# Moving the K, V and wq/wo slots below the constants in a decode-attention kernel

## The chip, the cores and the metric

The kernel runs on one core of a Trainium2 chip. The metric is the device time of one execution in microseconds (us), lower is better.

## What is computed

A decode step of a transformer block for 4 sequences with one token each, in bfloat16, with a width D of 640: attention over a cache of 4096 positions with 32 heads of 128, then a dense block with the Mish activation. Cut to what matters:

```python
q  = (layernorm(x) @ wq) as [4, 32, 1, 128]           # wq is 640 x 4096
p  = softmax(einsum("bhqd,bhkd->bhqk", q, k_cache) * 128**-0.5)
o  = einsum("bhqk,bhkd->bhqd", p, v_cache)             # caches are 4 x 32 x 4096 x 128
h  = x + o as [4, 1, 4096] @ wo                        # wo is 4096 x 640
f  = layernorm(h) @ w1 + b1                            # w1 is 640 x 1728
h2 = h + (f * tanh(log1p(exp(-|f|)) + max(f, 0))) @ w2 # w2 is 1728 x 640
```

The two caches are 134 MB each, read once. All the weights together are some 15 MB.

## The kernel before, in words

The attention is cut into 32 groups: group g is four heads (`hq = g // 4`) of one sequence (`b = g % 4`). The 128 partitions hold those four heads with 32 partitions each, and a partition holds 128 consecutive positions of its head (R = 128). So one group's K is a tile of 128 partitions with 128 x 128 bfloat16, which is one run of 32,768 bytes in each partition, and V has the same form. One DMA of 4096 KB loads such a tile (`load_kv`, L85 to L94, issued from the SP queue at L93); only the last group's K and V come in two halves.

For each group and each half of its positions, VectorE multiplies the K tile in place by the broadcast query in two passes (L334, in `mul_and_sum`), and TensorE adds up the products over the 128 columns with 32 matmuls against an identity (L341, 16 in each half). VectorE finishes the sum (L353) and TensorE, VectorE and ScalarE make the softmax (L360 to L391). Then TensorE multiplies V by the weights (`pv_moving`, L238 to L250, 32 matmuls at L242), one group behind. Between the groups stand the query projection (L185 to L211, for the first eight groups), the loads and products of wo (L426 to L434 and `project`, L311) and the bias. The order is written out by hand (`manual_schedule`, L73, and the loop from L394).

The K pool and the V pool have two slots each. The load of K for group g + 2 is issued when the multiplies and matmuls of group g have released their slot (L416), that of V for group g + 1 after L242 of group g - 1 (L422). All of them stand in one queue, SP's, in program order. wq and wo use one after the other the single slot of the pool `wbig` (L106 and L431, wo in four DMAs whose rows are 1280 bytes). After the last group, w1 and the larger part of w2 go into a slot of the K pool (L453 to L464), and a short chain of small operations makes the dense block and writes the output (L467 to L597).

Where a tile lies in a partition follows from the order in which the pools are made (L75 to L79): each pool begins where the one before it ends, and each tile is placed at the next multiple of 32 bytes. The first 16,384 bytes are reserved, four small built-in constants come next, and the first pool begins at byte 16,512. The pools come in the order `consts`, `wbig`, `work`, `kpool`, `vpool`, and the pool `mlp` is made last (L452). The built program before has these first bytes:

| tile | first byte in each partition | modulo 512 | modulo 64 |
|---|---|---|---|
| `ident` (L113) | 17,792 | 384 | 0 |
| `qbs` (L213), the broadcast query | 36,736 | 384 | 0 |
| wq/wo slot | 48,416 | 288 | 32 |
| K slots | 93,088 and 125,856 | 416 | 32 |
| V slots | 158,624 and 191,392 | 416 | 32 |

Of the kernel before, what the change touches and what calls it, by code (L numbers as in the profile page):

```python
# [9 lines left out]
BF16 = mybir.dt.bfloat16  # L10
# [6 lines left out]
def kernel(  # L17
# [54 lines left out]

    ctx.enter_context(tc.manual_schedule())  # L73

    consts = ctx.enter_context(tc.tile_pool(name="consts", bufs=1))  # L75
    wbig = ctx.enter_context(tc.tile_pool(name="wbig", bufs=1))
    work = ctx.enter_context(tc.tile_pool(name="work", bufs=2))
    kpool = ctx.enter_context(tc.tile_pool(name="kpool", bufs=KBUFS))
    vpool = ctx.enter_context(tc.tile_pool(name="vpool", bufs=VBUFS))  # L79

    x_rows = A_x.rearrange("b s d -> (b s) d")
    out_rows = out.rearrange("b s (c p) -> (b s c) p", p=128)
# [546 lines left out]
```

## Time and profile before

| what | value |
|---|---|
| median of three runs | 674.84 us (674.6 to 674.92) |
| the profiled execution, its own time | 674.36 us |
| its span, first to last instruction | 672.6 us |
| granted TensorE clock, mean | 0.935 |
| TensorE, VectorE, ScalarE busy | 566.7, 351.6, 112.2 us (84%, 52%, 17% of the span) |
| bytes read from HBM | 283.35 MB, 421 GB/s over the span |
| VectorE's longest single wait group: L334 for K loads | 222.8 us in 30 waits |

The profile gives busy times of the engines, the span cut into 40 slices, the DMA queues with their packets, the chain of waits that ended last, and groups of like instructions. A DMA is cut into packets, here one for each partition's contiguous run; the trace has a record of every packet with its start, its duration and its size. The share of a DMA queue is the time that its packets took as a share of 16 engines over the window, and can go slightly over 100% because one packet of an engine begins a little before the one before it ends.

### The profile page before, as it was taken

The numbers are of one execution on the slowest core, as the hardware profiler recorded it, in microseconds if no ns is written. First come the engines' busy times: TensorE is split into PE (matmuls) and PEld (weight loads), VectorE is DVE, ScalarE is ACT, GpSimd is POOL, SyncE is SP. The second block draws the span as 40 slices with busy tenths as digits, with TensorE's granted clock in tenths as the row PEclk, the third lists the DMA queues.
The fourth block names the chain that finished last, engine by engine and source line by source line (L and its number), as shares of the span: only waits on it lengthen the run. The fifth ranks groups of instructions, "written<-read, shape, count | busy, mean of one in ns | idle before, by whom it ended". The sixth has DMA issues, their size and how long they took to land.

```text
span 672.6 us, 7163 instructions
## 1 busy us (share of the span) xinstructions
PE 566.7 (84%) x3121; PEld 256.1 (38%) x3121; DVE 351.6 (52%) x304; ACT 112.2 (17%) x343; POOL 2.4 (0%) x13
## 2 busy tenths in 40 slices
PE   0589999899998896688999899879988799888985
PEld 0234444344443332233443344333433344333454
DVE  2475445455654356236654545665544566554642
ACT  0022122122210111011110111111111111101231
POOL 1000000000000000000000000000000000000000
PEclk9999999799998987878998899898999799898995
DMA  9999999999999999999999999999999999999995
GB/s 373 437 436 437 430 428 428 426 437 434 432 431 421 422 416 412 441 419 425 430 434 427 433 430 430 431 435 432 431 428 428 433 434 437 428 431 424 433 411 204
DMA packets 15191, 283.81 MB, mean 422 GB/s; under 512 B 1267, under 2 KB 5559, under 8 KB 6584
## 3 DMA queue, kind: packets, MB, share of 16 engines
q1 hardware_dynamic: 15152, 283.36, 98.8%
q8 instruction: 24, 0.39, 0.2%
q14 instruction: 7, 0.06, 0.0%
q10 hardware_dynamic: 8, 0.01, 0.0%
HBM read 283.35 MB, written 0.01 MB: 421 GB/s over the span
## 4 chain that ended last, share of the span: by engine, by line
DMA 43%; PE 37%; DVE 18%; issue 1%; ACT 1%; SPq 0%; DVEq 0%
DMA kt<-in_A_k_cache_dram 41%; PE s L341 19%; DVE kt L334 15%; PE p L242 11%; PE ot L256 3%; DMA vt<-in_A_v_cache_dram 3%; PE q_ps L188 1%; PE qb_ps L202 1%; DVE s_sb L353 1%; PE tr L366 1%; DVE mx L371 1%; ACT q_all L195 1%; PE h_ps L511 0%; PE l_ps L280 0%; PE y2T L573 0%
## 5 line engine op out<-in xcount | busy, mean ns | idle before, releaser
L334 DVE TENSOR_TENSOR kt<-kt,qbs 128x4096 bf16<-128x4096 bf16 x128 | 291.4, 2278 | 222.8 <-DMA kt<-in_A_k_cache_dram 222.8
L341 PE MATMUL s<-kt,ident 128*128 128x512 bf16 x1024 | 267.4, 408 | 75.8 <-DVE kt L334 75.6
L242 PE MATMUL p<-vt,e 128*16 128x512 bf16 x960 | 214.2, 382 | 0.0
L341 PEld LDWEIGHTS <-ident 128*128 128x128 bf16 x1024 | 99.7, 103 | 199.5 <-issue 100.6
L242 PEld LDWEIGHTS <-e 128*16 128x16 bf16 x960 | 84.3, 90 | 129.8 <-issue 17.8
L384 ACT ACTIVATE e<-s_sb,nbs 32x128 bf16<-32x128 f32 x128 | 73.9, 577 | 2.5
L250 ACT COPY p_sb<-p 16x512 f32<-16x512 f32 x30 | 17.2, 574 | 316.6 <-PE p L242 316.6
L353 DVE TENSOR_REDUCE s_sb<-s 128x64 f32<-128x512 f32 x64 | 43.4, 678 | 3.4 <-PE s L341 3.3
L381 ACT COPY nbs<-tr 128x4 f32<-128x4 f32 x32 | 5.2, 162 | 177.4 <-PE tr L379 177.4
L256 PEld LDWEIGHTS ot<-ident_f,p_sb 16*128 16x128 f32 x240 | 28.9, 186 | 12.7 <-issue 12.7
L384 ACT ACTIVATION_READ_ACCUMULATOR e<-s_sb,nbs 32x1 f32 x128 | 32.1, 251 | 0.0
L256 PE MATMUL ot<-ident_f,p_sb 16*128 16x4 f32 x240 | 31.5, 250 | 0.0
L371 DVE TENSOR_REDUCE mx<-tr 1x4 f32<-1x128 f32 x32 | 8.9, 277 | 41.4 <-PE tr L366 41.3
L188 PE MATMUL q_ps<-wq_sb,xT 128*4 128x512 bf16 x40 | 11.0, 409 | 9.7 <-DMA wq_sb<-in_A_wq_dram 9.7
L366 PE MATMUL tr<-ident_f,pm 128*1 128x128 f32 x64 | 13.7, 300 | 1.2 <-DVE pm L364 1.2
L379 PEld LDWEIGHTS tr<-mx,nscale 1*128 1x128 f32 x64 | 9.4, 182 | 13.8 <-issue 12.7
L288 DVE RECIPROCAL rl<-l_ps 128x16 f32<-128x16 f32 x8 | 2.1, 257 | 23.1 <-PE l_ps L280 23.1
L202 PE MATMUL qb_ps<-q_all,sel 4*128 4x128 bf16 x128 | 9.2, 225 | 5.3 <-ACT q_all L195 5.3
L379 PE MATMUL tr<-mx,nscale 1*128 1x4 f32 x64 | 12.2, 258 | 0.4 <-DVE mx L371 0.4
L202 PEld LDWEIGHTS <-sel 4*128 4x128 bf16 x128 | 8.4, 98 | 9.1 <-issue 9.1
L195 ACT CAST q_all<-q_ps 4x512 bf16<-4x512 f32 x8 | 4.6, 574 | 34.6 <-PE q_ps L188 34.6
L366 PEld LDWEIGHTS tr<-ident_f,pm 128*1 128x1 f32 x64 | 2.8, 81 | 18.4 <-issue 18.4
(79 smaller groups left out, 81.5 us busy)
## 6 DMA issues: line engine op xcount, KB each, us to landing
kt<-in_A_k_cache_dram SPq DMA_DIRECT2D x31, 4096.0 KB, 24.5
vt<-in_A_v_cache_dram SPq DMA_DIRECT2D x31, 4096.0 KB, 27.7
wq_sb<-in_A_wq_dram SPq DMA_DIRECT2D x1, 5120.0 KB, 15.3
wo_sb<-in_A_wo_dram SPq DMA_DIRECT2D x4, 1280.0 KB, 30.5
kt<-in_A_k_cache_dram SPq DMA_DIRECT2D x2, 2048.0 KB, 19.6
vt<-in_A_v_cache_dram SPq DMA_DIRECT2D x2, 2048.0 KB
w<-in_B_w_dram SPq DMA_DIRECT2D x1, 2160.0 KB, 22.9
w<-in_B_w_dram SPq DMA_DIRECT2D x3, 640.0 KB, 19.8
```

Source lines behind the costliest of these rows:

```text
L188: nc.tensor.matmul(q_ps[:, :], lhsT=xT[:, c, :], rhs=wq_sb[:, c, n * QC : (n + 1) * QC], start=(c == 0), stop=(c == DC - 1),)
L202: nc.tensor.matmul(qb_ps[:, b * Dh : (b + 1) * Dh], lhsT=sel[:, b, q, :], rhs=q_all[:, h * Dh : (h + 1) * Dh], start=(q == 0), stop=(q == ...
L242: nc.tensor.matmul(p_ps[:, :], lhsT=e2[g % NE2][:, r : r + J, :].rearrange("p j q -> p (j q)"), rhs=vt[:, r : r + J, :].rearrange("p j d - ...
L250: nc.scalar.copy(out=blocks[g][:, :], in_=p_ps[:, :])
L256: nc.tensor.matmul(o, lhsT=p_sb[:, j * Dh : (j + 1) * Dh], rhs=ident_f[0 : J * G, j * G : (j + 1) * G], start=(j == 0), stop=(j == J - 1),)
L334: nc.vector.tensor_tensor(out=kt[:, :, d0 : d0 + DQ], in0=kt[:, :, d0 : d0 + DQ], in1=qbs[:, hq, b, d0 : d0 + DQ].unsqueeze(1).to_broadcas ...
L341: nc.tensor.matmul(s_ps[:, :, :], lhsT=ident[:, :], rhs=kt[:, :, d : d + W], start=(d == 0), stop=(d == Dh - W),)
L353: nc.vector.tensor_reduce(out=s_sbs[g][:, part * RP : (part + 1) * RP], in_=s_of.pop((g, part))[:, :, :], axis=AX.X, op=ALU.add,)
L366: nc.tensor.matmul(tr_ps[0:1, 0:128], lhsT=pm[:, :], rhs=ident_f[:, :], start=True, stop=True)
L371: nc.vector.tensor_reduce(out=mx[:, :], in_=tr_ps[0:1, 0:128].rearrange("o (a b) -> o a b", a=G), axis=AX.X, op=ALU.max,)
L379: nc.tensor.matmul(nb_ps, lhsT=nscale[:, :], rhs=mx[:, :], start=True, stop=True)
L384: nc.scalar.activation(out=e2[g % NE2][p0:p1, :, q], in_=s_sb[p0:p1, :], func=ACT.Exp, bias=nb[p0:p1, q : q + 1], scale=SCALE, accum_out=r ...
```

## The change

Four things are done to the pools. An unused tile of 384 bytes in a new pool `pad` is made first. `kpool` and `vpool` follow, then `wbig`, then `consts`, then `work`; `mlp` is still the last. Nothing else is edited.

```diff
-    consts = ctx.enter_context(tc.tile_pool(name="consts", bufs=1))
-    wbig = ctx.enter_context(tc.tile_pool(name="wbig", bufs=1))
-    work = ctx.enter_context(tc.tile_pool(name="work", bufs=2))
+    pad = ctx.enter_context(tc.tile_pool(name="pad", bufs=1))
+    pad.tile([128, 192], BF16, name="pad")
     kpool = ctx.enter_context(tc.tile_pool(name="kpool", bufs=KBUFS))
     vpool = ctx.enter_context(tc.tile_pool(name="vpool", bufs=VBUFS))
+    wbig = ctx.enter_context(tc.tile_pool(name="wbig", bufs=1))
+    consts = ctx.enter_context(tc.tile_pool(name="consts", bufs=1))
+    work = ctx.enter_context(tc.tile_pool(name="work", bufs=2))
```

In the built program of the change the first bytes are these:

| tile | first byte in each partition | modulo 512 |
|---|---|---|
| K slots | 16,896 and 49,664 | 0 |
| V slots | 82,432 and 115,200 | 0 |
| wq/wo slot | 147,968 | 0 |
| `ident` | 190,208 | 256 |
| `qbs` | 209,152 | 256 |

## The prediction

> **What bounds the kernel now.** I read the DMA rows of the page first, since the kernel streams 283 MB and computes little on each byte. The first fence is the page: its two DMA lines in 40 slices, its SP queue, the loads of K and V.
>
> ```profile
> DMA  9999999999999999999999999999999999999995
> GB/s 373 437 436 437 430 428 428 426 437 434 432 431 421 422 416 412 441 419 425 430 434 427 433 430 430 431 435 432 431 428 428 433 434 437 428 431 424 433 411 204
> ...
> q1 hardware_dynamic: 15152, 283.36, 98.8%
> ...
> kt<-in_A_k_cache_dram SPq DMA_DIRECT2D x31, 4096.0 KB, 24.5
> vt<-in_A_v_cache_dram SPq DMA_DIRECT2D x31, 4096.0 KB, 27.7
> ```
>
> The 16 DMA engines are busy from the first slice to the last but one. A K load of 4096 KB needs 9.8 us at 430 GB/s, but lands 24.5 us after its issue: about 15 us of other loads stand ahead of it, so the queue doesn't run dry. The same by stages (columns: length; busy time and instructions of PE, PEld, DVE, ACT, POOL; granted clock; DMA share; GB/s):
>
> ```profile
> 26.00:44.00 18.00, 13.87 (x67) 5.84 (x67) 15.35 (x11) 1.16 (x2) 0.00 (x0) 1.00 1.00 433
> 50.00:125.00 75.00, 70.65 (x379) 32.51 (x378) 40.41 (x31) 16.87 (x48) 0.00 (x0) 1.00 1.00 429
> 330.00:600.00 270.00, 239.46 (x1167) 104.25 (x1166) 147.22 (x116) 42.73 (x140) 0.00 (x0) 0.95 1.00 431
> 656.00:672.00 16.00, 8.88 (x229) 8.24 (x229) 3.42 (x17) 2.00 (x4) 0.00 (x0) 0.50 0.57 208
> ```
>
> The DMA share is 1.00 wherever K and V stream, with VectorE busy for 15.35 of 18 us as well as with it half idle. Only from 656 us, after the last V, is it lower. Last, the chain of waits: early groups hold no DMA, one group following the other by TensorE at 19.2 us (50.60 to 69.81), so computing and DMA run at nearly one pace; later the chain waits for K.
>
> ```profile
> 50.60 7.00 PE p L242 x32
> ...
> 62.85 2.21 DVE kt L334
> 65.11 1.89 PE s L341 x8
> 66.99 0.98 PE ot L256 x8
> 67.97 1.83 PE s L341 x8
> 69.81 7.00 PE p L242 x32
> ```
>
> So the end is set by how long the 16 engines take over their packets, plus 16 us of tail.
>
> **The change, part by part.** *The programs.* In the built program of the change every engine has the same instructions in the same order with the same waits, SP's loads included; only addresses in SBUF differ. Nothing is moved past a queue, no wait is added, the unused tile takes no instruction. So only two prices can change: that of a packet's write, and that of an engine's read or write of a tile.
>
> *A packet's write.* K and V rows begin at 416 modulo 512 before and at 0 after; wq and wo at 288 before and 0 after. What does one packet cost beyond its bytes? The DMA view of 26 to 44 us, where the stream is undisturbed, says:
>
> ```profile
> DMA packets 267, 7.80 MB, mean 433 GB/s; under 512 B 29, under 2 KB 29, under 8 KB 29
> q1 hardware_dynamic: 267, 7.80, 100.3%
> ```
>
> 29 packets are the semaphores' (4 bytes, 9 ns each in the records of single packets), the other 238 are rows of 32,768 bytes: (1.003 x 16 x 18 us - 0.3 us) / 238 = 1,213 ns. The single records agree: until 44.7 us every row takes exactly 1,213 ns, and the 16,384-byte rows of the last halves take 611 ns at the least. The difference, 602 ns for 16,384 bytes, is 27.2 bytes per ns, so the bytes of a row alone need 1,204 ns. In one engine's sequence the next packet begins 1,210 ns after a row's start, 607 ns after a half row, 131.5 ns after a w1 row of 3,456 bytes (127 ns of bytes), and 6 ns after a semaphore packet. The cost beyond the bytes is 4 to 6 ns each time. It is no larger for the row that begins at 160 modulo 256 than for four bytes of semaphore, whose place the change doesn't touch. So I take the part that alignment could remove at **0 us**.
>
> The bound: all of some 5 ns goes. One engine has 7,936 / 16 = 496 whole rows, 512 / 16 = 32 half rows, 128 / 16 = 8 rows of wq, 4,096 / 16 = 256 of wo, and 40 + 24 of w1 and w2 (they lie in a K slot), together 856 packets; 856 x 5 ns = **4.3 us**, a gain of 0.64%. [...]
>
> The rows of w1 begin at 160 and 32 modulo 256 in turn, and the trace has runs of them at 135 ns each with starts 131 to 132 ns apart, whichever it is. [...]
>
> *Disturbed packets.* From 330 to 480 us whole rows take 1,218.6 ns on average, not 1,213. This begins with the first instruction load at 44.71 us and not with the computing, which starts at 25.87; in several stretches of single records every fourth packet of an engine is the long one, by some 7 ns, whatever its size. Neither speaks for a place in SBUF. I take no change. The 5.6 ns as a bound lie beside the 5 ns above: I don't add them.
>
> *The engines.* L334, L341 and L242 read the moved tiles. L334 has 2,278 ns for 4,096 columns, and the chain shows L341 at 1.83 us for 8 matmuls of 512 columns and L242 at 7.00 us for 32: 0.45 ns per column in the one, 0.43 in the other, though the first reads runs of 16 bytes at steps of 256 and the second whole rows. All start at a multiple of 32 bytes before and after. I take 0. The cover is the wait for K in the later groups (L334 waits 222.8 us for it) and, in the early ones, the 15 us of loads ahead of each load.
>
> *The tail.* Its small operations read constants and `mlp` tiles that lie elsewhere now; there is no DMA cover for them after 656 us. They have 8.88 + 3.42 + 2.00 = 14.3 us of busy time there. No row shows a dependence on the place, so 0; a tenth as a bound is 1.4 us either way.
>
> **Sum.** 0 on the profiled execution's 674.36 us (672.6 of span and 1.8 around it). The median of the runs shown is 0.48 above that execution; on the median, 674.8. About 0.2% (1.35 us) is what a measurement of this kernel can tell from no change.
>
> **The rivals.**
> - *A, forecast, no change:* 674.8, with 673.5 to 676.1 as its own range.
> - *B, aligned writes are cheaper.* For it: the engines are saturated, so every ns of a packet counts, 0.86 us of the end per ns. Against it: the 4-byte packets carry the same 6 ns. To pass 0.2% it needs 1.6 of the 5 ns. With three to four of them, 2.6 to 3.4 us are gained: about 671.8; at most 670.5.
> - *C, slower: L334's two reads collide.* Its inputs `kt` and `qbs` begin at 416 and 384 modulo 512 before, 32 bytes apart; after, at 0 and 256, so each pair of equal columns lies at the same place modulo 256. Were the two reads served one after the other, L334 would take twice as long: 128 x 2.28 = 291 us more on VectorE, 351.6 + 291.4 = 643 us busy. It starts at 25.9 and some 20 us of tail follow: 690 at least. It decides from the point where the 15 us of queued loads are used up in the eight early groups: with one L334 per group on the chain 1.8 us more each, with all four 0.46 us more (20%). Against it: no row of the trace shows two reads colliding, and L334 runs near half a ns per column.
> - *D, the tail or the constants get slower* by the tenth above: 676.3.
> - That the change doesn't do what it says is excluded by the first bytes in the built program, all multiples of 512.
>
> **How the numbers follow.** A 0.61, B 0.24, C 0.06, D 0.09. Faster by over 0.2% is B, within it A, slower C and D. The range runs from B's bound, 670.5, to D's, 676.3; C, and part of D, are left out.
>
> **What would show it.** In the profile after, undisturbed rows (26 to 44 us) again at 1,213 ns, 433 GB/s and share 1.00, L334 at 2,278 ns, L341 and L242 as above, and the end of the stream at 656 us. B would show in packets of 1,208 to 1,210 ns and a rate of 434 or 435 in that stretch. C would show in L334's duration alone, with the DMA share falling below 1.00. What would make me wrong without any of these is a place-dependent part in the disturbed packets, seen as a mean other than 1,218.6 ns between 330 and 480 us.

## The result and the profile after

The median fell from 674.88 to **671.26 us** (six executions each): 3.6 us less, a ratio of 0.9943 with a 95% interval of 0.9931 to 0.9956. The profiled execution of the change took 672.24 us, the longest of its six, with a span of 670.4 us; that of before took 674.36 with 672.6. The forecast, no change with 673.5 to 676.1, was not met. The gain has about the size of rival B, but it did not come the way B said.

The page of the change, its DMA rows, the loads of K and V, and VectorE's multiply (line numbers are 3 higher than before). The columns behind the bar in the multiply's line, L337, are busy time, mean ns of one, and the idle time before it with what ended it:

```profile
DMA  9999999999999999999999999999999999999994
GB/s 374 438 437 436 427 429 427 437 436 435 429 428 427 428 425 428 430 428 430 431 437 436 431 431 425 436 434 435 431 434 425 436 435 432 435 429 428 434 414 175
...
q1 hardware_dynamic: 15152, 283.36, 98.6%
...
L337 DVE TENSOR_TENSOR kt<-kt,qbs 128x4096 bf16<-128x4096 bf16 x128 | 291.4, 2279 | 211.6 <-DMA kt<-in_A_k_cache_dram 211.6
...
kt<-in_A_k_cache_dram SPq DMA_DIRECT2D x31, 4096.0 KB, 23.8
vt<-in_A_v_cache_dram SPq DMA_DIRECT2D x31, 4096.0 KB, 26.5
```

The DMA engines are as full as before (98.6% against 98.8%). The multiply takes the same time (2,279 ns against 2,278) but waits 11 us less for K (211.6 against 222.8). The slices in which the four loads of wo run, the 14th to the 16th and the 18th, moved 422, 416, 412 and 419 GB/s before and 428, 425, 428 and 428 now.

The same stages as before (length; PE, PEld, DVE, ACT, POOL busy; clock; DMA share; GB/s):

```profile
26.00:44.00 18.00, 13.83 (x63) 5.71 (x62) 14.78 (x9) 1.16 (x2) 0.00 (x0) 1.00 1.00 431
50.00:125.00 75.00, 70.65 (x378) 32.40 (x377) 40.42 (x31) 16.41 (x48) 0.00 (x0) 1.00 1.00 431
218.00:300.00 82.00, 63.26 (x275) 26.82 (x274) 37.58 (x30) 11.64 (x39) 0.00 (x0) 0.88 1.02 428
330.00:600.00 270.00, 236.82 (x1170) 104.25 (x1169) 149.80 (x119) 42.73 (x140) 0.00 (x0) 0.96 1.00 432
```

Before, the second of them had 429 GB/s and the last 431; the wo stage, 218 to 300 us, had 419. The first, which had 433, is not faster: its rows take 1,213 ns in both.

```profile
218.00:300.00 82.00, 62.86 (x268) 26.36 (x268) 37.66 (x30) 11.64 (x39) 0.00 (x0) 0.86 1.01 419
```

So the gain is a little on every row of K and V and more on the short rows of wo. The records of single packets tell it best. Between 330 and 480 us a whole row took 1,218.6 ns before and 1,214.9 now. Almost all rows are at the least value, 1,213 ns, which was true before only until about 45 us; what is left above it is a few rows of 1,460 to 1,760 ns beside instruction loads, and those were there before, too. Rows of wo went from 59.6 to 55.1 ns, where 55 is the least of most of them.

By the records the last V rows end at 655.8 us before and at 652.2 after, 3.6 us sooner. The tail behind them hasn't changed: from the last group of matmuls on V to the end it is 15.0 us before and 15.2 after, by the chain of waits (start, length, what; "issue" is time in which the engine waited for nothing that the profile shows); first before, then after:

```profile
638.66 17.60 DMA vt<-in_A_v_cache_dram
...
656.30 0.21 PE ot L268 x2
656.52 1.05 issue
657.57 1.81 PE ot L268 x62
...
667.37 2.20 PE y2T L573 x70
```

```profile
651.95 1.74 PE ot L271 x66
653.69 1.52 issue
655.21 1.81 PE ot L271 x62
...
665.25 2.20 PE y2T L576 x70
```

Between the two something did change. Before, TensorE waits for the last half of V; in the profile of the change it doesn't, because its own work reaches that half later than the data. In part for this, the span fell by 2.2 us and not by the 3.6 us that the stream gained. In o256 below, with a span of 668.7 us, TensorE doesn't wait there either.

### The profile page after: what moved, and what is told of

Its sections match the earlier page's. It is cut to its first block, busy times and chain, and to the rows that moved or that the text cites. A ratio compares the mean times of both kernels' runs of the same rounds, so it can differ in the third digit from the quotient of the medians.

```text
span 670.4 us, 7163 instructions
## 1 busy us (share of the span) xinstructions
PE 562.8 (84%) x3121; PEld 255.9 (38%) x3121; DVE 351.6 (52%) x304; ACT 112.2 (17%) x343; POOL 2.4 (0%) x13
## 3 DMA queue, kind: packets, MB, share of 16 engines
q1 hardware_dynamic: 15152, 283.36, 98.6%
## 4 chain that ended last, share of the span: by engine, by line
PE 45%; DMA 34%; DVE 19%; issue 1%; ACT 1%; SPq 0%; DVEq 0%
DMA kt<-in_A_k_cache_dram 34%; PE s L344 21%; DVE kt L337 16%; PE p L245 15%; PE ot L259 3%; PE q_ps L191 1%; PE qb_ps L205 1%; PE ot L271 1%; PE tr L369 1%; DVE mx L374 1%; DVE s_sb L356 1%; ACT q_all L198 1%; PE l_ps L283 0%; PE h_ps L514 0%; PE yT L318 0%
## 5 line engine op out<-in xcount | busy, mean ns | idle before, releaser
L337 DVE TENSOR_TENSOR kt<-kt,qbs 128x4096 bf16<-128x4096 bf16 x128 | 291.4, 2279 | 211.6 <-DMA kt<-in_A_k_cache_dram 211.6
L344 PE MATMUL s<-kt,ident 128*128 128x512 bf16 x1024 | 262.9, 404 | 77.1 <-DVE kt L337 77.0
L367 DVE TENSOR_REDUCE pm<-s_sb 128x1 f32<-128x128 f32 x32 | 9.2, 286 | 1.1
```

The source lines that it names most:

```text
L337: nc.vector.tensor_tensor(out=kt[:, :, d0 : d0 + DQ], in0=kt[:, :, d0 : d0 + DQ], in1=qbs[:, hq, b, d0 : d0 + DQ].unsqueeze(1).to_broadcas ...
L344: nc.tensor.matmul(s_ps[:, :, :], lhsT=ident[:, :], rhs=kt[:, :, d : d + W], start=(d == 0), stop=(d == Dh - W),)
```

## The experiments

Theory 1 says that the place of a row modulo some power of two sets what its packet costs; theory 2, that the low place or the order of the pools does; theory 3, that the constants and the engines' side do. Those that time the whole kernel were run in five rounds against the kernel before, the others give one profile. "Rows" are whole K or V rows. Their means are from the packet records of the whole run after 60 us, with the few rows over 1,240 ns, those beside instruction loads and wo rows, left out, so that they can be compared.

**Other offsets in the order of the change.** Only the size of the unused tile differs. Of o256, theory 1c says that a multiple of 256 is enough, theory 1d that 512 is needed:

```diff
-    pad.tile([128, 192], BF16, name="pad")
+    pad.tile([128, 208], BF16, name="pad")   # o32;  224: o64;  320: o256;  o128: no tile
```

o32: 

> The pool order of the change, but the unused tile has 416 bytes, so K, V and wq/wo begin at 32 modulo 512 (32 modulo 64). Theory 1 (packets to misaligned places are disturbed): the time is that of before, 674 to 675 us, and whole rows average about 1,218 ns between 330 and 480 us, with a spread from 1,213 to 1,226. Theory 2 (the low place, or the order of the pools, matters, not the multiple): 671 to 671.5 us and 1,214.6 to 1,215 ns, with nearly all rows at 1,213. Theory 3 (the constants and small tiles, on the engines' side, gained the time): 671 to 672 us with disturbed rows.

o64: 

> The pool order of the change, but the unused tile has 448 bytes, so K, V and wq/wo begin at 64 modulo 512. Theory 1 with a step of 64 bytes: 671 to 671.5 us, rows nearly all at 1,213 ns, the same as the change. Theory 1 with a step of 256 or 512 bytes: 673 to 675 us, rows average 1,216 to 1,219 ns. Theory 2: 671 to 671.5 us, as for 32.

o128: 

> The pool order of the change without the unused tile: K, V and wq/wo begin at 128 modulo 512. Offsets of 32 and 64 gave the time of before with disturbed rows, so the multiple that is needed is over 64 bytes. Theory 1a (a multiple of 128 is enough): 671 to 672 us, rows at 1,213 ns. Theory 1b (256 or 512 is needed): 674.5 to 675.5 us, whole rows 1,218 to 1,220 ns on average between 330 and 480 us.

o256: 

> The pool order of the change, but the unused tile has 640 bytes, so K, V and wq/wo begin at 256 modulo 512. [...] Theory 1d (512 is needed): 674.5 to 675.5 us with disturbed rows.

**One part alone in the order of before.** kv_high moves K and V alone to a multiple of 512, w_only the slot of wq and wo alone:

```diff
+    pad.tile([128, 48], BF16, name="pad")     # kv_high: ahead of kpool
...
+    pad.tile([128, 112], BF16, name="pad")    # w_only: ahead of wbig
+    pad2.tile([128, 16], BF16, name="pad2")   # w_only: ahead of kpool
```

kv_high: 

> The pool order of before, with an unused tile of 96 bytes ahead of the K pool: K and V begin at 0 modulo 512 above the constants, wq/wo stay at 288 modulo 512. Theory 1: of some 3.4 us gained the part of the K and V rows comes, about 2.0 to 2.5 us, so 672.3 to 673 us; whole rows at 1,213 ns, rows of wo (1,280 bytes) still 59 to 60 ns on average, not 55. Theory 2: 674.5 to 675 us, nothing gained.

w_only: 

> The pool order of before, with an unused tile of 224 bytes ahead of the wq/wo slot and one of 32 bytes ahead of the K pool: wq/wo begin at 0 modulo 512, K and V at 160 modulo 512 (32 modulo 64). Theory 1: the part of the wo rows comes, 256 rows in an engine by 4.4 ns, about 1.1 us, so 673.5 to 674 us; rows of wo at 55 ns, whole K and V rows still about 1,218.5 ns. Theory 2: 674.5 to 675 us.

What was measured (offsets of K and V and of wq/wo modulo 256; medians in us, each beside the kernel before on the same chip):

| kernel | K, V at | wq, wo at | time | before | ratio (95%) | rows, mean ns | rows at the least | wo rows, mean ns |
|---|---|---|---|---|---|---|---|---|
| before | 160 | 32 | 674.88 | | | 1,216.7 | 13% | 59.6 |
| the change | 0 | 0 | 671.26 | 674.88 | 0.9943 (0.9931 to 0.9956) | 1,213.0 | 100% | 55.1 |
| o256 | 0 | 0 | 671.00 | 675.23 | 0.9939 (0.9924 to 0.9954) | 1,213.0 | 100% | 55.1 |
| o128 | 128 | 128 | 674.66 | 675.23 | 0.9991 (0.9981 to 1.0000) | 1,216.9 | 22% | 59.2 |
| o64 | 64 | 64 | 675.61 | 675.00 | 1.0004 (0.9994 to 1.0013) | 1,216.8 | 6% | 59.4 |
| o32 | 32 | 32 | 675.38 | 675.00 | 1.0004 (0.9995 to 1.0013) | 1,217.9 | 6% | 59.6 |
| kv_high | 0 | 32 | 672.00 | 675.00 | 0.9957 (0.9941 to 0.9973) | 1,213.0 | 99% | 58.2 |
| w_only | 160 | 0 | 673.57 | 675.00 | 0.9980 (0.9970 to 0.9991) | 1,216.0 | 29% | 55.1 |

Theory 2 falls: the low place at an offset of 32, 64 or 128 gains nothing that the intervals tell from zero, and the high place at 0 gains 0.43%. Theory 3 falls with it. Of the offsets tried, the multiple that these rows need is 256 bytes: at 256 modulo 512 (o256) the kernel took 671.00 us with rows at 1,213.0 ns, at 128 it took 674.66 us with 1,216.9 ns and at 64 675.61 us with 1,216.8 ns. So 64 and 128 are not enough, and 512 is not needed. The parts add up: 0.43% for K and V (which takes w1 and w2 along, in a K slot) and 0.20% for wq and wo are 0.63%, against 0.57% for both. An aligned row isn't harmed by misaligned ones around it: wo rows average 55.1 ns in w_only, K and V rows 1,213.0 ns in kv_high.

**Is it in the DMA engines, or in what reads the tiles?** dma_only has all loads of before but the bias's 3.4 KB in the same order, at the same offsets modulo 512, and no computing; dma_pe adds TensorE work on two constant tiles; dma_al is dma_only with aligned slots.

```diff
-        (the multiplies, matmuls and softmax of the group)
+        pp = ps.tile([128, 512], FP32, tag="pp", bufs=2, name=f"pp{g}")   # dma_pe alone
+        for r in range(144):
+            nc.tensor.matmul(
+                pp[:, 0:320], lhsT=ident[:, :], rhs=fill[:, :], start=(r == 0), stop=(r == 143)
+            )
```

dma_only: 

> All loads at the offsets of before (K and V at 416, wq and wo at 288 modulo 512), in the same order, but all computing is left out and zeros are written; so hardly any instruction loads either. Theory 1e (the disturbance lies within the DMA engines' own writes): whole rows average 1,217 to 1,220 ns in the middle of the run. Theory 1f (it needs engines that read the tiles, or the instruction loads that knock the stream out of step): rows at 1,213 ns throughout.

dma_pe: 

> As dma_only, and TensorE runs 144 matmuls per group on two constant tiles, which never touch K or V but cause instruction loads as the real kernel has them. If rows are at 1,213 ns in dma_only and at 1,217 to 1,220 here, soon after the first instruction load, then an instruction load sets off the disturbance and reading the K and V tiles isn't needed. If they are at 1,213 ns in both, the engines' work on the tiles is needed. If they are disturbed in both, neither is.

dma_al: 

> As dma_only (loads alone, no computing, zeros written), but K, V, wq and wo begin at multiples of 512. Theory 1c: whole rows at 1,213 ns throughout, wo rows at 55 ns, and a span some 3 us below the 664.7 us of dma_only, about 661.5 to 662. If the cause were in what engines read, rows would stay at 1,217 ns on average.

The spans, dma_only and then dma_al, and their SP queue between 440 and 600 us (packets, MB, share of 16 engines):

```profile
core 0: 664.7 us, clock 1.000
```

```profile
q1 hardware_dynamic: 2366, 69.14, 100.4%
```

```profile
core 0: 661.1 us, clock 1.000
```

```profile
q1 hardware_dynamic: 2384, 69.24, 100.2%
```

A row's mean can be had from these lines: 69.14 MB are 2,110 rows, the other 256 packets are semaphores of 9 ns, and (1.004 x 16 x 160 us - 2.3 us) / 2,110 = 1,217.0 ns in dma_only. The same for dma_al, with 2,113 rows, gives 1,213 ns. With no engine at work and no instruction load but one, the misaligned rows are disturbed and the aligned ones not, and the whole difference of the kernel, 3.6 us, is there again. So theory 1e holds and 1f falls: the cost needs neither an engine that reads the tiles nor an instruction load, and the place that the packets are written to is all that differs between the two programs. dma_pe behaves likewise (1,219 ns with its rows beside instruction loads).

**What about the offset costs, the start or the number of blocks?** A block is here what lies between two neighbouring multiples of 256 bytes in a partition, 256 being the least multiple that gave clean rows above; how many blocks a row touches follows from its first byte and its length. Both kernels are dma_only with rows cut to 32,640 bytes; only the place differs, by an unused tile of 160 bytes ahead of the K pool in short64.

```diff
-            nc.sync.dma_start(out=t[:, r0:r1, :], in_=view[:, r0:r1, :])
+            n = (r1 - r0) * Dh - 64
+            nc.sync.dma_start(
+                out=t[:, r0:r1, :].rearrange("p r d -> p (r d)")[:, 0:n],
+                in_=view[:, r0:r1, :].rearrange("p r d -> p (r d)")[:, 0:n],
+            )
```

short160: 

> As dma_only, but each K and V row is loaded without its last 64 columns: 32,640 bytes, from 160 modulo 256, so that a row touches 129 blocks of 256 bytes where its length needs 128. Undisturbed it would take 1,208 ns. Theory 1g (a row is disturbed that touches one block more than its length needs) and theory 1h (a row is disturbed that doesn't begin at a multiple of 256) both say disturbed: 1,212 ns on average, few rows at the least value.

short64: 

> The same rows of 32,640 bytes (the last 64 columns left out) from 64 modulo 256: they end at 128 modulo 256 and touch 128 blocks, no more than their length needs. Theory 1g: undisturbed, nearly all rows at 1,208 ns, as when aligned. Theory 1h: disturbed, 1,212 ns on average.

The same window of the queue, short160 and then short64:

```profile
q1 hardware_dynamic: 2367, 68.90, 100.4%
```

```profile
q1 hardware_dynamic: 2397, 69.36, 100.4%
```

By the same sum a row takes (1.004 x 2,560 us - 2.3 us) / 2,111 = 1,216 to 1,217 ns in short160 (1,217.0 in the records) and 1,208 ns in short64 (1,208.0, with 99% of the rows at 1,208). Neither begins at a multiple of 256. (The rows of short64 end at 192 modulo 256, not at 128 as its expectation has it; they touch 128 blocks either way.) So theory 1h falls, and 1g holds: **what costs is one more block of 256 bytes touched than the length needs**. The expectation for short160 was too low, though: its rows lose not 4 ns but 9, and end at the same 1,217 ns as rows of 32,768 bytes that touch as many blocks.

The price of a block can be estimated from these rows. In the packet records of the change, the next packet of an engine begins 3 to 4 ns before the record of a row ends, so to the next start a whole row takes 1,209.5 ns of its 1,213, a wo row 51.8 of 55 and a w1 row 131.7 of 135; for the rows of short64, 1,208 ns less the same 3.5 are 1,204.5. A misaligned whole row, of 129 blocks, takes 4.0 ns more (dma_only less dma_al); 1,213.5 over 129 is an estimated 9.407 ns for each block touched, full or not. The excess by the estimate is that for all blocks of a row, less its time without the extra block. Since the 9.407 is from the first line of this table, only the other three test it:

| packets | without the extra block, to the next start | blocks with it, at 9.407 ns | excess by the estimate | measured excess |
|---|---|---|---|---|
| rows of 32,768 (dma_only less dma_al) | 1,209.5 | 129: 1,213.5 | 4.0 | 4.0 |
| rows of 32,640 (short160 less short64) | 1,204.5 | 129: 1,213.5 | 9.0 | 9.0 |
| wo rows of 1,280 (dma_only less dma_al) | 51.8 | 6: 56.4 | 4.6 | 4.6 |
| w1 rows of 3,456, 3 in 5 with 15 blocks (same) | 131.7 | 15: 141.1 | 9.4 x 3 / 5 = 5.6 | 5.8 |

In o128 the w1 rows begin at 128 and 0 in turn, touch 14 blocks either way, and 72% of them take the least time, while the K and V rows of that kernel are disturbed (1,216.9 ns on average). The 1 ns more in o32 the estimate doesn't explain. No row here is long in blocks and short in bytes, so the price of a block was not measured by itself, and what the engine does with a block was not shown; that rows with an extra block take longer is shown by short160 (1,217.0 ns) and short64 (1,208.0 ns).

**When does it set in?** v1_first issues one more load before the stream begins:

```diff
+    vts[1] = load_v(1)                 # after vts[0], ahead of the loop
...
-        if g + 1 < NG:
+        if g + 1 < NG and g > 0:
```

v1_first: 

> As dma_only, but the load of the second V tile is issued at the start with the first four, before the stream runs. In every misaligned kernel so far the rows of the loads issued in the first microseconds (wq, two K, one V) took 1,213 ns, and the disturbance set in at about 44 us, with the load that was issued next. Theory 2a (only loads issued into a running stream are disturbed): undisturbed to 53 us. Theory 2b (it sets in at a time or a number of bytes): 44 us again.

Theory 2a falls: the disturbance sets in at 47.4 us (the first time that 8 of 16 rows in a row are over the least), as in dma_only. Up to then an engine has had 27.4 rows after the 8 of wq in dma_only, 12.6 in short160, and 36.1 in w_only, where wq is aligned. An estimate of what these rows would have lost later in the stream, with 4 ns for each misaligned row (wq's too) and 9 for the K and V rows of short160, comes to 142, 145 and 144 ns. The same count gives 142 and 141 ns in o64 and v1_first, but 113 in o32 (20.3 rows) and 159 in o128 (31.8), so these are not one number. What sets the onset was not shown.

The records of wo bear on it. From a fifth to two fifths through the first wo load, rows average 55.0 ns in kv_high and short64, where K and V are clean, but 58.5 before and 60.1 in dma_only. In the three later loads the same stretch takes 57.0 to 57.6 in kv_high and 59.7 to 59.8 in short64. So misaligned wo rows, too, begin clean where little came before them that touched a block too many; kv_high's wo rows average 58.2 ns, under the 59 to 60 expected, which fits. All this was seen after the fact, and no run was made to test it.

## Why the prediction was right or wrong, step by step

- **What bounds the kernel** was right for the stream: the DMA share stayed at 1.00, and a few ns per packet moved its end by 3.6 us. What follows the stream is TensorE's: in the profile of the change it no longer waits for the last V.
- **The forecast**, no change, was wrong. That 671.26 lies inside the whole range is owed to rival B's bound, which set the lower end, and not to the mechanism that was forecast.
- **"A packet's write", 0 us.** The undisturbed rows before 44.7 us were read rightly, and up to 38 us they are 1,213 ns at every offset of the whole kernels. But they were taken as the price of a misaligned write, and they are that price in the first 45 us or so only: from 47.5 us on they are longer. That a row at 160 touches 129 blocks and an aligned one 128 was given no price; that it has one is shown by short160 and short64 (1,217.0 against 1,208.0 ns).
- **"Disturbed packets. [...] Neither speaks for a place in SBUF. I take no change": this is the step that failed.** Of the 5.6 ns by which rows exceeded 1,213 between 330 and 480 us, 3.7 went with the place; the remaining 1.9 are the rows beside instruction loads. The onset beside the first instruction load, at 44.71 us, was a coincidence: dma_only has no such load until 627 us, and the rows are disturbed from 47.4 us there and from 47.5 before, by the measure used above. The pattern of every fourth packet was wrongly taken to exclude the place; why each fourth is the long one stays open.
- **The wo rows** stood in the bound, but were not looked at by themselves. Their mean of 59.6 ns against a least of 55 was in the records. They are 256 x 4.5 ns = 1.15 us of an engine; K and V are 496 x 4 + 32 x 4 = 2.1 us, the w1 rows 0.2 us. Together 3.5 us, and 3.6 were measured.
- **The bound** of 5 ns for 856 packets, 4.3 us, held by luck: it was a packet's own cost beyond its bytes, which isn't what was lost. By kind of row the loss is 4 to 6 ns here, but 9 in short160.
- **Rival B** had nearly the price (2.6 to 3.4 us) but not the way: rows at 1,208 to 1,210 ns before 44 us didn't appear, and that stretch is unchanged. The case that came is the one in the last sentence of "What would show it".
- **The row of w1**, "135 ns each [...] whichever it is", was read from runs of single records, which misled: only 11% of the w1 rows before took 135 ns, and they average 145 (84% and 138 in the profile of the change). Nor does the loss grow with the offset: K and V rows at 32, 64, 128 and 160 modulo 256 average 4.9, 3.8, 3.9 and 3.7 ns over the least (o32, o64, o128, before), and those of short160, which have 32 bytes in their last block, lose 9 ns.
- **Engines, tail, C and D**: 0 was right for each. L334 (L337 after) stayed at 2,278 to 2,279 ns, and the tail at 15 us.

## What to carry to other kernels

In a stream that keeps the DMA engines full, try a place for each SBUF destination where no row touches one block of 256 bytes more than its length needs; here, with the DMA queue at 98.6% to 98.8%, that was worth 0.6% with rows of 32 KB, and the short rows gained most for their bytes (4.5 of 59.6 ns). Look at the spread of single packets late in the stream, against the least value and by kind of row, before calling a packet's price fixed: up to 38 us the rows of the whole kernels took 1,213 ns at every offset. A bound over all packets gave the size of this change without its cause, but only because the unknown loss was about as large as the cost that was bounded.

## What was not expected of the hardware

Rows that touch a block too many take the least value all the same for the first 12.6 (short160) to 36.1 (w_only) K or V rows of an engine, and then most are longer: after 60 us, 13% of them are at 1,213 ns before. The other surprise is what an instruction load is worth: dma_pe, whose TensorE work never touches K or V and causes 36 loads of 16 KB, has a span of 671.5 us against 664.7 in dma_only. Whole rows beside such a load take 1,680 to 1,764 ns in its records, so these rows are held up beside the loads (1,213 ns is the least). That these loads alone make the 6.8 us wasn't tested.
